# A new fixed order of the work in an attention and Hyena kernel on one Trainium2 core

## Chip, cores and metric

The kernel runs on one core of one Trainium2 chip. The metric is the device time of one execution in microseconds; smaller is better. Engines are named as in the profile: PE (TensorE, the matrix engine) with PEld (its weight loads), DVE (VectorE), ACT (ScalarE), POOL (GpSimd) and SP (SyncE, which here only issues DMAs).

## The reference

Softmax attention with one added to the denominator ("off by one"), then a Hyena layer on the joined heads. All inputs and outputs are float32; 8 batches, 12 heads, 448 positions, 64 values per head, so D = 768.

```python
def _attn_ref(q, k, v):
    scores = scale * np.matmul(q, k.transpose(0, 1, 3, 2))
    m = np.max(scores, axis=-1, keepdims=True)
    e = np.exp(scores - m)
    attn = e / (np.sum(e, axis=-1, keepdims=True) + np.exp(-m) + 1e-09)
    return np.matmul(attn, v)

def _moe_ref(x, w_proj, filter_fft, w_out):
    proj = x @ w_proj                       # [8, 448, 768] @ [768, 2304]
    x1, x2, x3 = proj[..., :D], proj[..., D:2 * D], proj[..., 2 * D:]
    X2 = np.fft.rfft(x2, n=S, axis=1)
    H = np.fft.rfft(filter_fft, n=S, axis=0)[None, :, :]
    x2_conv = np.fft.irfft(X2 * H, n=S, axis=1)
    return (x1 * x2_conv * x3) @ w_out
```

## The kernel before

**Attention.** Two heads are a group; 48 groups, six for each batch, numbered g = 0 to 47. For a group PE makes the scores (L842, the last 64 keys L844), ACT takes the exponentials (L855, L861), PE multiplies with the values (L873, L881), DVE divides by the sums (L894, L896) and leaves `xb`, which is transposed to `xT`: for batch 0 on PE (L978), for the others by a DMA.

**Loads.** SP issues the loads of q, k and v, POOL casts them to bf16. The last 64 keys and values of all twelve heads of a batch come in one load for each of k and v, the *shared* keys and values, named `rests` (L484 for batches 0 and 1, L619 for the others; runs of 256 bytes). Batches 0 and 1 are *staged*: loads at L467 (q) and L472 (k, v), casts at L494 (k), L500 (q), L507 (v), L522 (shared keys, `ks`) and L527 (shared values), then transposes on PE (L533 for the shared keys, L535 for the others, L542 for the query), copied back by DVE or, for group 6, the first of batch 1, by ACT (L550, L561). Batches 2 to 7 are *loaded*: L633 and L654, casts, and DMA transposes of q and k (L603, L610).

**Weights.** They are loaded by DMAs that POOL issues and thus stand in POOL's queue among its casts: the filter (L736, L737, L740), the projection in four parts (L820: x1's 1152 KB, the two halves of x2's of 576 KB each, x3's of 1152 KB) and the output weights (L825).

**Hyena layer, per batch.** x2's projection for batches 0 to 2 is L1070. For batches 3 to 7 it is *turned*: matmuls L1092, copies back on DVE (L1103) and ACT (L1105), a DMA transpose (L1109); then the spectrum matmuls L1142 read the transposed tile. The product with the filter's spectrum is on DVE (L1160, L1166). The gates x1 and x3 are L1192 on PE, with ACT's cast L1204 and DVE's product L1207; the inverse transform is L1238, with L1247, L1256, L1258, L1267; the gated y is L1282 (`yT`, `yR`), and the output matmuls are L1006, copied by ACT (L1314) and stored by SP (L1322, L1325, L1328).

**The flag.** A check of all batches for scores too large ends in a matmul L1407 and a copy L1409; at L1547 every engine reads the result and branches. A fixed set of output tasks is kept back to be run after the branch, in the same program.

**What sets the order.** The whole kernel but the setup is given to a planner, class `Plan`, as 2034 tasks: engine, modelled cost, needs, buffers. The planner simulates the engines and the DMA queues, and so decides the order in which each engine's instructions are written, and which PSUM banks they take. If `plan.ORDER` is given, a task's place among its engine's tasks is the number that stands for it in that list, and the simulation may no longer reorder an engine's queue:

```python
want = self.ORDER[len(self.tasks)] if self.ORDER else want + self.SHIFT.get(part, 0.0)
...
for i, t in enumerate(queue[e][: 1 if self.ORDER else self.WINDOW]):
    if ready(t):
        break
```

The number `run` of a DMA task is its weight when the two issuing queues share the DMA engines in the simulation: a transfer goes on at `run / total` of the speed, where `total` sums over the two transfers at the heads of the queues. Weight DMAs have 52 to 115, loads of q, k and v have 50, transposes 0.2.

Between the modelled times of 3 and 36 us the planner also fills modelled gaps of PE with matmuls on a tile of zeros (L1484, *fillers*; 78 of them). 38 more (L1492) run at the start.

Of the kernel before, what the change touches and what calls it, by code (L numbers as in the profile page):

```python
# [41 lines left out]
class Plan:  # L42
# [35 lines left out]
    def add(self, eng, cost, want, emit, need=(), make=(), take=(), give=(), dma=0.0, run=256, n=1, after=0.0, begun=(), late=0.0, turn=False, part=None, keep=False, port=False):  # L78
        want = self.ORDER[len(self.tasks)] if self.ORDER else want + self.SHIFT.get(part, 0.0)
        self.tasks.append((want, len(self.tasks), eng, cost, emit, need, make, take, give, dma, after, run, n, begun, late, turn, keep, port or eng == "POOL" and not dma))  # L80
# [221 lines left out]
def kernel(  # L302
# [93 lines left out]
    def stage(g, at, n):  # L396
        o = g % 4 * ROOM + at
        return nf[:, o : o + n]


    plan = Plan(
        {
            "e": 6, "er": 2, "k0": 2, "q0": 2, "u": 1, "w": 1, "xf": 1,
            "x2": 1, "x2s": 1, "x2h": 1, "xs": 2, "t0": 2, "t1": 2, "yh": 1, "g": 1, "x1": 2, "cr": 2, "cw": 1, "cv": 2, "yT": 1, "yR": 1,
            "os": 3,
        }
    )
# [25 lines left out]
    def tau(i, frac=0.0):  # L433

        if i >= NHP * n_batches:
            return tau(i - 1, frac + 1)
        h = i % NHP + frac
        return ATT[i // NHP] + SLOT[i // NHP] * min(h, 3) + LATER[i // NHP] * max(h - 3, 0)
# [4 lines left out]
    def rows(x, b, hp):  # L443
        o = x[b, 2 * hp].offset
        return bass.AP(x.tensor, o, [[3 * DH, 128], [512 * DH, 2], [1, 3 * DH]])

    def shared(x, b):
        o = x[b].offset + 384 * DH
        return bass.AP(x.tensor, o, [[DH, 128], [2 * S * DH, NHP], [1, DH]])

    def staged(b):
# [3 lines left out]
        for hp in range(NHP):  # L455
# [6 lines left out]
            for n, (name, x, at, size) in enumerate(parts):  # L462
                src = stage(g, at, size)

                def load(name=name, x=x, src=src, hp=hp, g=g):
                    if name == "q":
                        (nc.sync if g else nc.scalar).dma_start(  # L467
                            src[0:SP].rearrange("p (u c) -> p u c", u=2),
                            q[b, 2 * hp : 2 * hp + 2].rearrange("u (p j) d -> p u (j d)", j=NST),
                        )  # L470
                    else:
                        nc.sync.dma_start(  # L472
                            src.rearrange("p (u c) -> p u c", u=2), rows(x, b, hp)
                        )

                need = [("c" + name, g - 4)] if g >= 4 else []
                old = g - 2 * NHP
                first = name == "q" and g == 0
                add("ACT" if first else "SP", 0.52 if first else 0.5, -21.0 if first else want + 0.1 * n, load, need=need,
                    make=[("s" + name, g)], after=hold, dma=0.92 if name == "q" else 0.69, run=50,  # L480
                    begun=[("i" + name, g)])
                if hp == 0 and name != "q":
                    add("SP", 0.5, want + (0.05 if name == "k" else SLOT[0] + 0.05) if b == 0 else want - RE1 + 0.1 * n,
                        lambda name=name, x=x: nc.sync.dma_start(rests[:, "kv".index(name)], shared(x, b)),  # L484
                        need=[("cr" + name, b - 1)] if b else (), make=[("r" + name, b)],
                        dma=1.14, run=50, begun=[("ir", b)])

                on_pool = g > 0
                eng = nc.gpsimd if on_pool else nc.vector

                def cast(name=name, src=src, hp=hp, g=g, eng=eng):
                    if name == "k":
                        T[g]["kn"] = t = k0s[g % 2]
                        eng.tensor_copy(  # L494
                            t.rearrange("p j (u d) -> p u j d", u=2),
                            src.rearrange("p (u j d) -> p u j d", u=2, j=3),
                        )
                    elif name == "q":
                        T[g]["qn"] = t = q0s[g % 2]
                        eng.tensor_copy(  # L500
                            t.rearrange("p j u d -> p u j d"),
                            src[0:SP].rearrange("p (u j d) -> p u j d", u=2, j=NST),
                        )
                    else:
                        sv = src.rearrange("p (u j d) -> p u j d", u=2, j=3)
                        for u in range(2):
                            nc.gpsimd.tensor_copy(  # L507
                                vn[b % 2][:, hp, 4 * u : 4 * u + 3, 0:DH], sv[:, u]
                            )

                T.setdefault(g, {})
                if name == "v":
                    add("POOL", 0.62, tau(g) + (1.0 if b == 0 else -4.0), cast,
                        need=[("sv", g)] + ([("V", old, 1)] if b >= 2 else []), make=[("cv", g), ("v", g)])
                else:
                    add("POOL" if on_pool else "DVE", (0.47 if name == "k" else 0.58) if on_pool else 0.42, tau(g) - 5.0, cast, port=True,
                        need=[("s" + name, g)] + ([("c" + name, g - 1)] if g else []), make=[("c" + name, g)], take=[(name + "0", g)])
            if hp == 0:
                for u in range(2):
# [5 lines left out]
                        need=[("rk", b), "zero ks"] + ([("T", NHP * b - 1 - h) for h in range(NHP)] if b else []), make=[("crk", b)])  # L525
                add("POOL", 0.56, tau(g) + 1.0,
                    lambda: nc.gpsimd.tensor_copy(vn[b % 2][:, :, 3, 0:DH], rests[:, 1]),  # L527
                    need=[("rv", b)], make=[("crv", b), ("vr", b)])
# [65 lines left out]
    def loaded(b):  # L594
# [22 lines left out]
        for n, (name, x) in enumerate((("k", k), ("v", v))):  # L617
            add("SP", 0.5, tau(i0) - lead[0] - 0.2 + 0.1 * n,
                lambda name=name, x=x: nc.sync.dma_start(rests[:, "kv".index(name)], shared(x, b)),  # L619
                need=[("cr" + name, b - 1)], make=[("r" + name, b)], dma=1.14, run=50)  # L620
        for u in range(2):
            c = slice(64 * u, 64 * u + 64)
            add("POOL", 0.52, tau(i0) - lead[1] - 0.2, lambda c=c: nc.gpsimd.tensor_copy(kn[c, :, 0, c], rests[c, 0]),
                need=[("rk", b)] + (["zero kn"] if b == NSTAGED else [("kT", i) for i in range(i0 - NHP, i0)]), make=[("crk", b)])
        add("POOL", 0.52, tau(i0) - lead[3], lambda: nc.gpsimd.tensor_copy(vn[b % 2][:, :, 3, 0:DH], rests[:, 1]),
            need=[("rv", b), ("V", i0 - NHP - 1, 0), ("V", i0 - NHP - 1, 1)], make=[("crv", b), ("vr", b)])

        for hp in range(NHP):
# [8 lines left out]
                need=[("cq", g - QS)] if n >= QS else [("cq", i0 - 1)] if n == 0 else [], make=[("sq", g)], dma=0.92, run=50)  # L637
# [5 lines left out]
                need=[("sq", g)] + ([("qT", g - NHP)] if b > NSTAGED else staged_done), make=[("cq", g)])  # L643
            if hp % few == 0:
                gs = range(g, g + few)
                add("SP", (1.22, 1.42)[few > 1], tau(g) - lead[6], lambda hp=hp: q_turn(hp), need=[("cq", i) for i in gs] + last,
                    make=[("qT", i) for i in gs], dma=(0.7, 1.43)[few > 1], run=0.2, late=-0.2, turn=True)
            for n, (name, x) in enumerate((("k", k), ("v", v))):
# [6 lines left out]
                    need=room, make=[("s" + name, g)], dma=0.69, run=50)  # L655
                sv = src.rearrange("p (u j d) -> p u j d", u=2, j=3)
                if name == "k":
# [4 lines left out]
                        need=[("sk", g)] + (["zero kn"] if b == NSTAGED else [("kT", g - NHP)]), make=[("ck", g)])  # L662
                    if hp % few == 0:
                        gs = range(g, g + few)
                        add("SP", (1.22, 1.42)[few > 1], tau(g) - lead[2], lambda hp=hp: k_turn(hp), need=[("ck", i) for i in gs] + [("crk", b)] + last,
                            make=[("kT", i) for i in gs], dma=(0.78, 1.49)[few > 1], run=0.2, late=-0.2, turn=True)
# [798 lines left out]
    with (  # L1465
# [48 lines left out]
        for b in range(n_batches):  # L1514
            if b < NSTAGED:
                staged(b)
            else:
                loaded(b)
        add("DVE", 0.5, tau(NHP * NSTAGED) - 30.0, lambda: nc.vector.memset(kn[:, :, 0, :], 0.0),
            need=[("c" + x, g) for x in "kqv" for g in range(NHP * NSTAGED - NHP, NHP * NSTAGED - 2)], make=["zero kn"])  # L1520
        for (part, ch), at in zip(LOADS, LOAD):
# [4 lines left out]
            elif ch is None:  # L1526
                add("POOL", 0.82, at, lambda part=part: wproj_load(part, None), make=[("w", part, 0), ("w", part, 1)], dma=4.9,
                    run=60, late=-0.34, after=at)
# [6 lines left out]
        for b in range(n_batches):  # L1535
# [3 lines left out]
            need=[("T", NHP * NSTAGED - 1), ("T", NHP * NSTAGED - 2)], make=["x2h pads"])  # L1539
# [6 lines left out]
    with (  # L1546
# [6 lines left out]
        for b in range(n_batches):  # L1553
            W["yT", b], W["yR", b // 2] = y, yr
            stable(b)
            plan = Plan(plan.size)
# [9 lines left out]
    with tc.manual_schedule(engines={E.PE, E.Pool, E.DVE, E.Activation, E.SP}):  # L1566
        plan = main
# [31 lines left out]
```

## Time and profile before

| | us |
|---|---|
| median of 3 runs | 383.2 |
| lowest and highest | 382.7, 383.39 |
| the profiled execution | 381.13 |
| its span | 379.4 |
| PE busy | 364.5 (96%) |
| ACT busy | 264.0 (70%) |
| DVE busy | 260.4 (69%) |
| POOL busy | 111.8 (29%) |

The mean granted clock of PE in the profiled execution is 0.988 of full speed. The page and the views of the trace come from this one execution. In groups of instructions the numbers stand in this order: count (x), busy time in us, mean ns of one instruction from its start to its end (matmuls overlap, so busy time divided by the count is what one adds), idle time ahead of them on the engine and what ended it. In the timeline a row has the start, the length, the engine, the line, the operation and in brackets the idle time ahead with its releaser. Queue positions below are counted in the instructions as compiled.

### The profile page before, as it was taken

How to read it: one execution, taken by the hardware profiler on the slowest of the kernel's cores; microseconds unless marked ns; L12 is line 12 of the kernel's file. 1: busy time of each engine (PE TensorE's matmuls, PEld its weight loads, DVE VectorE, ACT ScalarE, POOL GpSimd, SP SyncE). 2: the span in 40 equal slices, each digit the busy share in tenths (PEclk: the TensorE clock that was granted, in tenths of full speed). 3: DMA queues.
4: the chain of work that ended last, by engine and by line, in shares of the span. 5: the costliest groups of instructions: out<-in, count | busy, mean ns of one | idle time of the engine just before them, and what ended most of it. 6: DMA issues, size and time to landing. Idle time of an engine off the chain costs nothing. (4 is left out here: it accounts for less than half of the span.)

```text
span 379.4 us, 9372 instructions
## 1 busy us (share of the span) xinstructions
PE 364.5 (96%) x3622; PEld 219.4 (58%) x3622; DVE 260.4 (69%) x676; ACT 264.0 (70%) x455; POOL 111.8 (29%) x240
## 2 busy tenths in 40 slices
PE   8878999999999999999999999999989999999995
PEld 6656666556755675655465545655545555555553
DVE  6465778966699668684685778695476855748770
ACT  4884887776877767886687567777868875446343
POOL 4834632423533373364116232430023000000000
PEclk9996999999999999999999999999999999999998
DMA  8999994999989999999999999997664044433035
GB/s 214 255 237 248 233 227 98 173 170 216 216 192 259 219 271 215 238 167 248 215 199 272 224 172 219 278 211 160 99 182 113 11 58 112 124 84 85 1 129 169
DMA packets 132450, 68.41 MB, mean 180 GB/s; under 512 B 88813, under 2 KB 129200, under 8 KB 132400
## 3 DMA queue, kind: packets, MB, share of 16 engines
q1 hardware_dynamic: 127680, 62.11, 73.1%
q0 software_dynamic: 4480, 5.41, 8.4%
q8 instruction: 29, 0.48, 0.5%
q10 hardware_dynamic: 240, 0.23, 0.2%
q14 instruction: 21, 0.17, 0.1%
HBM read 43.86 MB, written 11.01 MB: 145 GB/s over the span
## 5 line engine op out<-in xcount | busy, mean ns | idle before, releaser
L855 ACT ACTIVATE e<-psum 128x896 bf16<-128x896 f32 x144 | 128.3, 922 | 20.9 <-PE psum L842 18.9
L1192 PE MATMUL psum<-xT,wproj_bf 128*128 128x448 bf16 x576 | 122.1, 352 | 0.4 <-DVE g L1207 0.4
L1192 PEld LDWEIGHTS <-wproj_bf 128*128 128x128 bf16 x576 | 54.1, 98 | 45.8 <-issue 2.8
L1006 PE MATMUL psum<-wout_bf,yT 128*128 128x384 bf16 x288 | 53.1, 326 | 0.4 <-DVE yT L1282 0.4
L881 PE MATMUL psum<-vn,e 128*128 128x65 bf16 x1152 | 47.6, 195 | 0.0
L639 POOL CAST nat<-nat 112x512 bf16<-112x512 f32 x36 | 24.2, 674 | 73.7 <-DMA nat<-in_q_dram 70.4
L881 PEld LDWEIGHTS <-e 128*128 128x128 bf16 x1152 | 42.4, 98 | 5.2 <-issue 0.2
L1204 ACT CAST x<-psum 128x448 bf16<-128x448 f32 x48 | 25.5, 537 | 23.9 <-PE psum L1192 22.3
L842 PE MATMUL psum<-qT,kT 64*128 64x448 bf16 x288 | 41.2, 357 | 0.6 <-ACT e L855 0.4
L1160 DVE TENSOR_TENSOR t<-xs,hrs 113x768 bf16<-113x768 bf16 (+1 forms) x64 | 36.5, 592 | 6.4 <-ACT xs L1154 6.3
L1154 ACT CAST xs<-psum 113x384 bf16<-113x384 f32 (+1 forms) x64 | 29.2, 487 | 16.3 <-PE psum L1142 13.5
L1207 DVE TENSOR_TENSOR g<-x,psum 128x448 bf16<-128x448 bf16 x48 | 29.5, 617 | 15.9 <-PE psum L1192 12.2
L1314 ACT COPY osb<-psum 128x384 f32<-128x384 f32 x54 | 25.1, 486 | 19.7 <-PE psum L1006 14.9
L1006 PEld LDWEIGHTS <-yT 128*128 128x128 bf16 x288 | 27.1, 98 | 19.9 <-DVE yT L1282 1.9
L1092 PE MATMUL psum<-xf,wproj_bf 128*128 128x452 bf16 x180 | 38.6, 356 | 0.0
L896 DVE TENSOR_TENSOR xb<-psum,den 128x512 bf16<-128x512 f32 x48 | 33.2, 691 | 1.7
L894 DVE TENSOR_SCALAR den<-psum 128x8 f32<-128x8 f32 x48 | 7.8, 164 | 33.9 <-PE psum L881 26.3
L671 POOL CAST vn<-nat 128x192 bf16<-128x192 f32 x58 | 23.2, 432 | 26.0 <-DMA nat<-in_v_dram 26.0
L861 ACT ACTIVATE er<-psum 128x448 bf16<-128x448 f32 x48 | 26.2, 553 | 6.8 <-PE psum L844 6.1
L1247 ACT CAST cr<-psum 128x452 bf16<-128x452 f32 x48 | 24.6, 546 | 6.4 <-PE psum L1238 5.9
L1070 PE MATMUL psum<-wproj_bf,xf 128*113 128x384 bf16 x144 | 26.2, 327 | 0.0
L1092 PEld LDWEIGHTS <-wproj_bf 128*128 128x128 bf16 x180 | 16.5, 96 | 16.1 <-issue 1.1
(129 smaller groups left out, 471.5 us busy)
## 6 DMA issues: line engine op xcount, KB each, us to landing
nat<-in_q_dram SPq DMA_DIRECT2D x47, 224.0 KB, 4.9
out_dram<-osb SPq DMA_DIRECT2D x21, 384.0 KB, 3.4
nat<-in_k_dram SPq DMA_DIRECT2D x41, 192.0 KB, 4.2
nat<-in_v_dram SPq DMA_DIRECT2D x41, 192.0 KB, 3.9
wproj_bf<-in_moe_w_proj_dram POOLq DMA_DIRECT2D x2, 1152.0 KB, 15.7
out_dram<-osb SPq DMA_DIRECT2D x12, 192.0 KB, 2.8
rests<-in_k_dram SPq DMA_DIRECT2D x8, 192.0 KB, 4.4
rests<-in_v_dram SPq DMA_DIRECT2D x8, 192.0 KB, 4.4
```

The costliest lines, as they stand in the source:

```text
L842: nc.tensor.matmul(sc[:, u, 0:S], kT[b % 2][c, hp, t, :], qT[b % 2][c, hp, :])
L855: nc.scalar.activation(to, of, AF.Exp, scale=SCALE)
L861: nc.scalar.activation(to, of, AF.Exp, scale=SCALE)
L881: nc.tensor.matmul(out_bank(u)[:, n, :], P["e"][1 + t][:, u * S + n * 128 : u * S + n * 128 + 128], vn[b % 2][:, hp, 4 * u + t, :], start= ...
L896: nc.vector.tensor_tensor(W["xb", b][:, hp].rearrange("p n (u d) -> p u n d", u=2), op[:, :, :, 0:DH], rec[:].unsqueeze(3).to_broadcast([1 ...
L1006: nc.tensor.matmul(ops[:n, :DCH], y[:, dt, 0:n], wout_bf[:, dt, ch * DCH : (ch + 1) * DCH], start=(dt == 0), stop=(dt == NDT - 1),)
L1070: nc.tensor.matmul(pps[:FQ, :DCH], W["xf", b][:, pg, kt, 0:FQ], wproj_bf[:, kt, D + ch * DCH : D + (ch + 1) * DCH], start=(kt == 0), stop= ...
L1092: nc.tensor.matmul(pps, wproj_bf[:, kt, D + dt * 128 : D + (dt + 1) * 128], W["xf", b][:, :, kt, 0:FQ], start=(kt == 0), stop=(kt == NDT - 1),
L1154: nc.scalar.copy(L["xs", par, ch][:K, pg % 2, :], L["Z", pg, ch][:K, :DCH])
L1160: nc.vector.tensor_tensor(t[:K], L["xs", par, ch][:K], h, op=ALU.mult)
L1192: nc.tensor.matmul(p[:, :S], wproj_bf[:, kt, 2 * part * D + dt * 128 : 2 * part * D + (dt + 1) * 128], xT()[:, kt, 0:S], start=(kt == 0), ...
L1207: nc.vector.tensor_tensor(g[:, dt, :], L["x1", dt], p[:, :S], op=ALU.mult)
```

## The change

Two things change. `plan.ORDER` is another list: 2034 numbers for the same tasks, nearly all of them different. And `run` goes from 50 to 22 for the loads of the shared keys and values, in both functions that make them. As the order is fixed, `run` has no say in it; it changes only the simulated times, by which banks and fillers are placed. The tasks, tiles, buffers and their sizes are the same. The new program has 61 fillers instead of 78.

```diff
-    plan.ORDER = (5, 9, 12, 826, 13, 17, 0, 6, 23, 8, 24, 38, 1, 11, 162, 2, 10, 25, ...
+    plan.ORDER = (8, 0, 12, 277, 7, 9, 1, 4, 26, 11, 18, 20, 5, 48, 226, 10, 13, 24, ...
...
                         need=[("cr" + name, b - 1)] if b else (), make=[("r" + name, b)],
-                        dma=1.14, run=50, begun=[("ir", b)])
+                        dma=1.14, run=22, begun=[("ir", b)])
...
-                need=[("cr" + name, b - 1)], make=[("r" + name, b)], dma=1.14, run=50)
+                need=[("cr" + name, b - 1)], make=[("r" + name, b)], dma=1.14, run=22)
```

What the new order does to the instructions of each engine, from the two compiled programs:

- SP, head: batch 1's shared keys go from 19th to 18th load, group 6's query from 20th to 21st, group 5's keys from 16th to 17th; the bytes are the same.
- POOL, head: the first two loads of L820 (x1's 1152 KB and x2's first 576 KB) come after ten casts instead of six, right behind the cast of group 5's keys. The other two loads of L820, neighbours before, are separated by a memset, three casts and L527.
- PE, head: 16 of batch 0's transposes L978 stand ahead of group 6's transposes instead of 4, and 13 fewer fillers.
- PE, batches 3 to 7: other matmuls are put between a half's last L1092 and its first L1142, more of them than before in nine of ten halves.
- PE, end: 14 matmuls of L1006 stand between L1407 and the branch.
- ACT, head: the load of the Exp table stands ahead of the first copy of the transposed keys.

2 lines of the change are left out of this document (1 added, 1 removed).

## The prediction

> **What bounds the kernel now.** I read the page first (busy shares, the slices, the clock), then TensorE's waits, then the head of the program in stretches as long as the clock's own steps, then its instructions there.
>
> ```profile
> PE 364.5 (96%) x3622; PEld 219.4 (58%) x3622; DVE 260.4 (69%) x676; ACT 264.0 (70%) x455; POOL 111.8 (29%) x240
> ...
> PEclk9996999999999999999999999999999999999998
> ```
>
> TensorE (PE) works for 364.5 of 379.4 us, and no other engine passes 70%. So a reordering can win only in two places: the 14.9 us in which PE does nothing, and the slice near 30 us in which its clock is 0.6 instead of 0.9 or more. Who is to blame for the first stands in PE's waits (total, times, longest):
>
> ```profile
> PE psum L542 <- POOL ldm L500: 2.1, 4, 0.8
> PE psum L533 <- POOL ks L522: 1.9, 1, 1.9
> PE psum L1142 <- DMA x<-nat: 1.3, 1, 1.3
> PE psum L1492 <- DVE idle L1480: 1.1, 1, 1.1
> PE psum L873 <- DVE g L1207: 0.8, 2, 0.4
> PE psum L1142 <- DMA x<-ldm: 0.7, 1, 0.7
> ```
>
> Two families stand out: PE transposes of shared keys and queries in the head (L533, L542), and the spectrum matmuls L1142, which wait for a DMA transpose of x2. The head by stretches (length, busy time of each engine, granted clock, DMA share, GB/s):
>
> ```profile
> core 0: us, PE busy (x) PEld busy (x) DVE busy (x) ACT busy (x) POOL busy (x), PEclk, DMA share, GB/s
> 8.70:12.10 3.40, 2.30 (x34) 1.81 (x32) 1.54 (x4) 2.92 (x7) 2.43 (x7) 1.00 1.16 264
> ...
> 25.80:29.20 3.40, 1.39 (x19) 0.85 (x16) 2.23 (x5) 2.66 (x5) 1.30 (x2) 1.00 1.14 234
> 29.20:32.60 3.40, 2.65 (x28) 1.97 (x28) 0.15 (x1) 1.02 (x2) 1.48 (x4) 0.50 1.22 233
> 32.60:36.00 3.40, 3.40 (x39) 2.36 (x33) 3.33 (x8) 2.27 (x3) 1.54 (x3) 0.50 1.17 272
> ```
>
> Between 25.8 and 29.2 PE works 1.39 of 3.40 us; for the two stretches behind it the clock is 0.50. A stretch with 2.30 of 3.40 busy is not followed by that. So PE loses 2.01 + 0.75 = 2.76 us idle, and then does 2.65 + 3.40 = 6.05 us of work at half speed, which at full speed is half as much: 3.0 us more. The head has 5.8 us to give. What it waits for, by the timeline:
>
> ```profile
> 16.75 1.72 POOL L820 DMA_DIRECT2D wproj_bf<-in_moe_w_proj_dram  x2
> ...
> 19.01 0.52 POOL L494 CAST ldm<-nat 128x384 bf16<-128x384 f32 x1
> ...
> 27.72 1.36 POOL L522 CAST ks<-rests 64x384 bf16<-64x384 f32 x2 [5.86 <-DMA rests<-in_k_dram]
> ...
> 29.14 0.27 PE L533 MATMUL psum<-ident_bf,ks 128*128 128x128 bf16 x1 [1.94 <-POOL ks L522]
> ...
> 30.48 0.55 PE L542 MATMUL psum<-ident_bf,ldm 112*128 112x112 bf16 x4 [0.75 <-POOL ldm L500]
> ...
> 37.46 1.64 POOL L820 DMA_DIRECT2D wproj_bf<-in_moe_w_proj_dram  x2
> ...
> 42.41 2.12 PE L1070 MATMUL psum<-wproj_bf,xf 128*113 128x384 bf16 x12
> ```
>
> Batch 1's shared keys land late (issued at 13.56, 14.0 us), because from 16.75 two projection weights are in flight beside them, from the other queue (KB, us from issue to landing):
>
> ```profile
> wproj_bf<-in_moe_w_proj_dram POOLq DMA_DIRECT2D x1, 1152.0 KB, 14.2
> ...
> wproj_bf<-in_moe_w_proj_dram POOLq DMA_DIRECT2D x1, 576.0 KB, 18.5
> ...
> rests<-in_k_dram SPq DMA_DIRECT2D x1, 192.0 KB, 14.0
> ...
> wproj_bf<-in_moe_w_proj_dram POOLq DMA_DIRECT2D x1, 1152.0 KB, 17.3
> wproj_bf<-in_moe_w_proj_dram POOLq DMA_DIRECT2D x1, 576.0 KB, 10.2
> ```
>
> **The head, step by step.** The new order puts the first two weight loads (L820) behind the cast of group 5's keys, now the 17th load of SP's queue, before the 16th. Here that cast is the L494 at 19.01, with 1.72 us of L820's issuing ahead of it on POOL. It could end earlier by that, were its load not one place later and more casts ahead of it: I put the issue of L820 at 19 to 22, middle 20.2 (an estimate from those rows), against 16.75. Batch 1's shared keys go from 19th to 18th on SP, the query of group 6 (batch 1's first) from 20th to 21st.
>
> What that gives the loads: 3.4 us without the weights, at 234 GB/s of which I count half as theirs (an estimate), is 0.40 MB more for SP's queue, two loads of 192 KB at 0.8 us each. So keys and query land about 2 us sooner: the keys by 25.6 instead of 27.56, and the casts of 1.36 + 0.61 us behind them end at about 28, instead of 30.42. On PE's side, 12 more of batch 0's transposes now stand ahead of group 6's, and 13 fewer of the idle filler matmuls:
>
> ```profile
> L978 PE MATMUL psum<-ident_bf,xb 128*128 128x128 bf16 x24 | 2.6, 250 | 0.0
> ...
> L1484 PE MATMUL psum<-idle 128*128 128x128 bf16 x78 | 6.4, 223 | 0.0
> ```
>
> 12 x 2.6/24 = 1.3 us of useful work more against 13 x 6.4/78 = 1.1 us of filling less. So of the 2.76 us of idle time at most one is left, in one stretch of the clock, and the clock stays. As the fillers stand only in time that is otherwise idle, the 17 fewer of the whole program save nothing.
>
> By this PE would be up to 5.8 us early. But the L1070 at 42.41 needs the second weight load. Before, the pair took 0.87 (half of L820's 1.72, the second being issued after the first) + 18.5 = 19.4 us from 16.75, landed at 36.1, and nothing waited for it; the later pair, from 37.46, took 0.8 + 17.3 = 18.1 us. An issue at 20.2 plus 18.1 to 19.4 is 38.3 to 39.6, with the issue's ends 37.1 to 41.4. I take L1070 at 39.0, the middle: 3.4 us sooner, bounds 1.0 and 5.3. What is late next is thus this weight, no longer the keys; it costs 1 us for each microsecond of issue. The other weight loads now go out apart, with casts of queries between them, so the next query needn't queue behind both; the page shows no wait for them before, and I count nothing.
>
> **The transposes of x2.** In batches 3 to 7 the projection of x2 is turned: L1092, a copy back, a DMA transpose, then L1142. Where it came late:
>
> ```profile
> 182.38 0.37 PE L1142 MATMUL psum<-x,ft 113*112 113x384 bf16 x1 [0.69 <-DMA x<-ldm]
> ...
> 277.11 0.37 PE L1142 MATMUL psum<-x,ft 113*112 113x384 bf16 x1 [1.30 <-DMA x<-nat]
> ...
> L842 PE MATMUL psum<-qT,kT 64*128 64x448 bf16 x288 | 41.2, 357 | 0.6 <-ACT e L855 0.4
> ...
> L881 PE MATMUL psum<-vn,e 128*128 128x65 bf16 x1152 | 47.6, 195 | 0.0
> ...
> L1092 PE MATMUL psum<-xf,wproj_bf 128*128 128x452 bf16 x180 | 38.6, 356 | 0.0
> ...
> L1192 PE MATMUL psum<-xT,wproj_bf 128*128 128x448 bf16 x576 | 122.1, 352 | 0.4 <-DVE g L1207 0.4
> ```
>
> The new order puts more of PE's other work between the last L1092 of a half and its first L1142. In batch 3's first half, for one, 6 more L1092 and 12 more L881: 6 x 38.6/180 + 12 x 47.6/1152 = 1.3 + 0.5 us. In batch 5's second half 6 more L1192 and 4 more L842: 6 x 122.1/576 + 4 x 41.2/288 = 1.3 + 0.6 us. Every half of batches 3 to 7 but one gains between 1 and 4 us; the exception, batch 6's second, has over 10 left. The two waits, 0.69 and 1.30 us, are smaller than the added cover: 2.0 us less. Bounds 0.5 (if the transposes themselves take longer behind a busier queue) and 2.0.
>
> **What else moves.** In the middle the other engines' queues keep nearly the same sequence: 0, within 1 us either way (PE's two waits for L1207 sum to 0.8 and could double or go). At the end, the flag matmul has only 14 L1006 between it and the branch:
>
> ```profile
> 360.35 0.16 PE L1407 MATMUL psum<-one,bad 128*1 128x1 bf16 x1
> ...
> 369.98 2.18 PE L1006 MATMUL psum<-wout_bf,yR 128*128 128x384 bf16 x12
> ```
>
> Here 9.6 us lie between the two and PE doesn't stop; 14 x 2.18/12 = 2.5 us must now cover the flag's way. No row times it: it costs between 0 and 9.6 - 2.5 = 7.1 us. I take 0, as one number's copy and reading is short beside 2.5 us; the far end is the third rival's.
>
> **Sum:** 3.4 + 2.0 = 5.4 us less. The profiled execution took 381.13 us (span 379.4 and 1.7 around it), so 375.7 in its frame; it lies 2.1 us under the median of 383.2, from which I forecast 377.8. Own range: 374.9 (head 5.3, turns 2.0, the middle 1.0) to 382.7 (head 1.0, turns 0.5, the middle losing 1.0); these ends together are unlikely, and I give it 375.5 to 381.
>
> **Rivals.**
> First, *the clock falls again, now ahead of L1070*. If PE is done early and waits 2 us or more for the weight, the stretch looks like 25.80:29.20, and 6 us of work at half speed cost 3.0 again: the head nets only 0.4 us, the turns stay, 383.2 - 0.4 - 2.0 = 380.8. For it: PE could be there at 42.4 - 5.8 = 36.6, 2.4 us before the weight. Against: the idle time must fall into one stretch of 3.4 us, and 12 transposes plus fillers are to be run in it. The stretch with 2.01 us idle says that two microseconds are enough. [...] Chance 0.14.
>
> Second, ending slower: *the weights become the wait*. With the head's 17 loads slower than I reckon, POOL's queue, which is in order, holds L820 behind casts that wait. From an issue at 42.41 - 18.7 + 2.0 = 25.7 on, the turns' gain is used up; at 27, L1070 comes at 45.7, 3.3 us late, with a long idle time ahead of it and so 3.0 us of half clock behind it: 383.2 + 3.3 + 3.0 - 2.0 = 387.5; without the clock's fall 384.5. For it: POOL waited 5.86 us for a load in this very stretch. Against: that load stood three places behind the one that counts, which was there by 19.01. Chance 0.18.
>
> Third, also slower: *the flag's way or a new wait in the middle* takes 6 us or so (up to 7.1): 383.2 - 5.4 + 6 = 383.8. Against: nothing on PE waits there now. Chance 0.09.
>
> Fourth, *nothing comes of it*: gains and new waits cancel, 383. Chance 0.05.
>
> **The numbers.** The forecast keeps 0.54. A measurement of this kernel tells about 0.2%, 0.77 us, from no change. Faster: 0.54 + 0.12 of the first rival = 0.66; same: 0.02 + 0.05 = 0.07; slower: 0.27. The range goes from 375.3, nearly the forecast's outer end, to 385, which takes in the first, third and fourth rivals and the milder half of the second.
>
> **What would show it.** Right: L533 and L542 of group 6 without a wait of over 1 us, clock 1.00 from 26 to 40 us, L820 issued at 19 to 22, L1070 at 37.1 to 41.4, no L1142 waiting for a DMA. Wrong: a clock of 0.50 anywhere before 45 us, PE idle over 2 us ahead of L1070 or a first L1192 for want of weights, L820 after 24, waits for L1547 on PE, or new waits for `xT<-xb` or x2 after 100 us.

## The result

| | old order | new order |
|---|---|---|
| median, us | 383.2 (5 runs, 382.04 to 384.15) | 376.37 (5 runs, 375.65 to 377.04) |
| profiled execution, us | 381.13 | 376.26 |
| its span, us | 379.4 | 374.5 |
| its mean granted clock | 0.988 | 0.997 |

The ratio is 0.9825, with a 95% interval of 0.98 to 0.9851. The forecast was 377.8 in a range of 375.3 to 385.

The page after (busy time by engine, the clock in 40 slices):

```profile
PE 359.4 (96%) x3605; PEld 216.4 (58%) x3605; DVE 260.8 (70%) x676; ACT 262.2 (70%) x455; POOL 109.6 (29%) x240
...
PEclk9999999999999999999999999999999999999999
```

PE is still the bound. It is busy for 5.1 us less, though it has only 17 matmuls fewer, fillers of 1.4 us; most of the rest is what the old program's work at half speed had cost (3.0), and the slice of 0.6 is gone. PE's waits (total, times, longest):

```profile
PE psum L844 <- ACT e L855: 1.8, 2, 1.6
PE psum L1006 <- ACT osb L1314: 1.4, 1, 1.4
PE psum L535 <- POOL ldm L494: 1.2, 2, 0.8
PE psum L1492 <- DVE idle L1480: 1.1, 1, 1.1
PE psum L978 <- DVE xb L896: 1.0, 2, 0.6
PE psum L842 <- DMA kT<-nat: 0.7, 1, 0.7
```

No L533 and no L1142 is left in it. The two largest in their place are waits that the old trace did not have: L844 for an exponential, and L1006 for an output copy behind the branch.

The head, as windows of the same times as before:

```profile
25.80:29.20 3.40, 2.61 (x32) 1.70 (x32) 3.09 (x9) 2.84 (x5) 1.20 (x2) 1.00 1.15 233
29.20:32.60 3.40, 3.40 (x57) 2.35 (x56) 2.87 (x10) 3.13 (x6) 1.00 (x3) 1.00 1.20 213
32.60:36.00 3.40, 3.31 (x49) 2.00 (x45) 2.93 (x11) 2.63 (x7) 1.67 (x5) 1.00 1.23 222
```

The clock is 1.00 throughout. What keeps the mean at 0.997 lies behind PE's last matmul, which ends at 369.1: from 372.5 to the end of the trace the clock stands at 0.50 with nothing for PE to do. A mean clock therefore says little about a single fall of 3.4 us, and the stretches are read instead wherever a trace is at hand. POOL's queue, and PE at the step for which the second weight load is needed:

```profile
18.59 1.73 POOL L820 DMA_DIRECT2D wproj_bf<-in_moe_w_proj_dram  x2
...
22.14 1.06 POOL L522 CAST ks<-rests 64x384 bf16<-64x384 f32 x2
```

```profile
37.33 2.11 PE L1070 MATMUL psum<-wproj_bf,xf 128*113 128x384 bf16 x12
```

L1070 begins at 37.33 instead of 42.41. So the head gave 5.1 us. How long this lead holds can be read by laying the two traces side by side at equal amounts of useful PE work (fillers left out): 5.1 us at the end of the head, 4.6 at 150 us, 5.5 just ahead of 200 us, 3.5 behind the wait at L844, 4.9 at 260, 6.4 behind the place of the old second L1142 wait, 7.5 at 362 us. The span is only 4.9 shorter: the last 2.6 us were lost again behind the branch.

### The profile page after: what moved, and what is told of

Read it like the earlier page. It is cut to its first block, busy times and chain, and to the rows that moved or that the text cites. A ratio compares the mean times of both kernels' runs of the same rounds, so it can differ in the third digit from the quotient of the medians.

```text
span 374.5 us, 9317 instructions
## 1 busy us (share of the span) xinstructions
PE 359.4 (96%) x3605; PEld 216.4 (58%) x3605; DVE 260.8 (70%) x676; ACT 262.2 (70%) x455; POOL 109.6 (29%) x240
## 5 line engine op out<-in xcount | busy, mean ns | idle before, releaser
L1192 PE MATMUL psum<-xT,wproj_bf 128*128 128x448 bf16 x576 | 121.9, 352 | 0.2 <-DVE ldm L1103 0.2
L1192 PEld LDWEIGHTS <-wproj_bf 128*128 128x128 bf16 x576 | 54.0, 98 | 48.3 <-issue 4.6
L1006 PE MATMUL psum<-wout_bf,yT 128*128 128x384 bf16 x288 | 54.0, 326 | 0.2 <-DVE yT L1282 0.2
L881 PE MATMUL psum<-vn,e 128*128 128x65 bf16 x1152 | 46.7, 194 | 0.0
L881 PEld LDWEIGHTS <-e 128*128 128x128 bf16 x1152 | 41.3, 98 | 5.0 <-issue 0.6
L1160 DVE TENSOR_TENSOR t<-xs,hrs 112x768 bf16<-112x768 bf16 (+1 forms) x64 | 36.6, 601 | 10.8 <-ACT xs L1154 10.8
L842 PE MATMUL psum<-qT,kT 64*128 64x448 bf16 x288 | 41.1, 355 | 1.2 <-DMA kT<-nat 0.7
L1092 PE MATMUL psum<-xf,wproj_bf 128*128 128x452 bf16 x180 | 38.6, 356 | 0.0
L1006 PEld LDWEIGHTS <-yT 128*128 128x128 bf16 x288 | 27.2, 98 | 19.1 <-DVE yT L1282 1.1
L1204 ACT CAST x<-psum 128x448 bf16<-128x448 f32 x48 | 25.6, 536 | 15.9 <-PE psum L1192 15.1
L639 POOL CAST nat<-nat 112x512 bf16<-112x512 f32 x36 | 23.6, 663 | 40.4 <-DMA nat<-in_q_dram 28.7
L671 POOL CAST vn<-nat 128x192 bf16<-128x192 f32 x58 | 21.7, 404 | 38.2 <-DMA nat<-in_v_dram 33.3
L1247 ACT CAST cr<-psum 128x452 bf16<-128x452 f32 x48 | 24.4, 547 | 8.2 <-PE psum L1238 6.4
L1070 PE MATMUL psum<-wproj_bf,xf 128*113 128x384 bf16 x144 | 26.4, 327 | 0.0
L1092 PEld LDWEIGHTS <-wproj_bf 128*128 128x128 bf16 x180 | 16.4, 96 | 16.6 <-issue 1.5
```

The lines of the kernel that those rows point to most:

```text
L842: nc.tensor.matmul(sc[:, u, 0:S], kT[b % 2][c, hp, t, :], qT[b % 2][c, hp, :])
L881: nc.tensor.matmul(out_bank(u)[:, n, :], P["e"][1 + t][:, u * S + n * 128 : u * S + n * 128 + 128], vn[b % 2][:, hp, 4 * u + t, :], start= ...
L1006: nc.tensor.matmul(ops[:n, :DCH], y[:, dt, 0:n], wout_bf[:, dt, ch * DCH : (ch + 1) * DCH], start=(dt == 0), stop=(dt == NDT - 1),)
L1070: nc.tensor.matmul(pps[:FQ, :DCH], W["xf", b][:, pg, kt, 0:FQ], wproj_bf[:, kt, D + ch * DCH : D + (ch + 1) * DCH], start=(kt == 0), stop= ...
L1092: nc.tensor.matmul(pps, wproj_bf[:, kt, D + dt * 128 : D + (dt + 1) * 128], W["xf", b][:, :, kt, 0:FQ], start=(kt == 0), stop=(kt == NDT - 1),
L1160: nc.vector.tensor_tensor(t[:K], L["xs", par, ch][:K], h, op=ALU.mult)
```

## The experiments

Orders are described by what moves; in the code each is another list of 2034 numbers. Each kernel ran beside the old program, whose median is given with it (382.4 to 383.1). An execution of the old program took between 379.7 and 386.4 us, so a difference of less than a microsecond in medians of four executions says little, and less still between kernels that were measured in different series; where the text reads a wait, it is from the kernel's one profiled execution.

**run22: the share numbers alone.**

```diff
# old order; both places
-  dma=1.14, run=50
+  dma=1.14, run=22
```

> The old order with only the two share numbers changed (run = 22), so that at most the banks and the fillers differ. If the order does it all: 383.2, within 0.8, with the clock at 0.50 for some 7 us behind 29 us and a mean of 0.98 to 0.99. If the share numbers matter by the fillers they place: under 382. The executions' clocks also say whether the old program's 2.1 us between its profiled execution and its median lie in the clock: then the slower executions have a lower mean clock.

Measured: 381.37 (10 executions) against 382.91, ratio 0.9948 (0.9903 to 0.9994). By the time alone that is the second expectation (under 382), 1.5 us less than the old program; by the clock of the profiled execution (0.989) it is the first. The trace has 23 matmuls more than the old program, all fillers, and the executions a mean clock of 0.995 in their median against 0.991. The waits at L533 and L542 stand where they stood (1.5 and 1.6 us), and the clock still falls to 0.50 for 6.8 us in the profiled execution. So the new share numbers may give a small part, which the forecast had at nothing; rest_new, which has them too, gained nothing. The order does the rest.

**head_new and rest_new: the two halves alone.**

```diff
# head_new: tasks with a new number under 310 in the new order, the others behind them in the old
# rest_new: tasks with an old number under 310 in the old order, the others behind them in the new
```

> The new order up to its 310th task (about the first 45 us), the old one behind it. Theory (the head gives 5.1 us, the rest nets next to nothing, because 2.4 us won at L1142 and elsewhere are lost again at the flag): 378.1, or 376 if the old program's executions lose up to 2 us more in the head than the profiled one. L1142 waits of 0.5 to 1.3 us near 180 and 275 us remain. Rival (turns and middle carry most): above 380.

> The old order for its first 310 tasks, the new one behind. Theory: the wait for the shared keys and the half clock are back; L1142 has no wait; the flag costs 2.5 us at the end: 382.5 to 383.4. Rival (the turns' 2 us come through to the end, the flag being free): 381.2 or less.

Measured: head_new 379.09 (4 executions), ratio 0.9872 (0.9797 to 0.9946); rest_new 383.08 (10 executions), ratio 1.0018 (0.9984 to 1.0053). Both are within 1 us of what the theory said: the head alone wins, the rest alone nothing. PE's longest waits in head_new, where the old turns meet a PE that is early:

```profile
PE psum L978 <- DVE xb L896: 1.8, 3, 1.0
PE psum L1142 <- DMA x<-ldm: 1.6, 1, 1.6
PE psum L1142 <- DMA x<-nat: 1.4, 1, 1.4
```

and of rest_new:

```profile
PE psum L1006 <- ACT osb L1314: 2.5, 1, 2.5
PE psum L542 <- POOL ldm L500: 2.2, 3, 1.4
PE psum L844 <- ACT e L855: 1.9, 1, 1.9
```

The halves sum to 3.6 us, the whole is worth 6.5 to 6.8. In the profiled executions head_new keeps a lead of 3.0 us of the 4.7 that it has behind the head: the two waits at L1142 grew from 2.0 to 3.0 us, and an L1192 waited 1.0. The new rest is thus worth more behind the new head than alone. Why the two turns wait longer there stays open; run22, with the same old turns, waited only 0.2 us at L1142, so part of it is the spread of the executions.

**old_w_later: only the first two weight loads moved, in the old order.**

```diff
# POOL, old order
-  ... cast q(3), L820, L820, cast q(4), cast k(5), ...
+  ... cast q(3), cast q(4), cast k(5), L820, L820, ...
```

> The old order with only the first two projection loads (L820) moved on POOL from behind group 3's query to behind the cast of group 5's keys, two casts later; SP's order is the old one. Theory (these weights beside the shared keys make the keys late): L820 issued near 18, the keys 1 to 1.5 us sooner, less half clock, 1.5 to 3 us less than the old program's 382.9: 380 to 381.4. Rival (the keys' place behind group 6's keys, and the filter's load, make them late): L533's wait stays at 1.0 to 1.9 us, 382.4 or more.

Measured: 377.16 (4 executions) against 383.06, ratio 0.9871 (0.9801 to 0.9941); the profiled one 376.40. That is more than was expected, and nearly the whole gain by moving two instructions past two. L820 went out at 18.66 instead of 16.75, the shared keys landed at 23.6 instead of 27.6, group 6 no longer waited for them, and L1070 began at 37.99. The clock was 1.00 in the head, and the stretch that had 2.01 us idle has 0.07:

```profile
25.80:29.20 3.40, 3.33 (x52) 2.21 (x49) 3.01 (x8) 3.40 (x7) 1.45 (x3) 1.00 1.14 229
29.20:32.60 3.40, 3.27 (x46) 2.40 (x46) 3.33 (x8) 2.60 (x6) 2.13 (x3) 1.00 1.18 232
```

The old waits at L1142 (0.7 and 1.2) are all there.

**new_w_sooner: the same two loads moved back, in the new order.**

```diff
# POOL, new order
-  ... cast q(4), cast k(4), cast q(5), cast v(2), cast k(5), L820, L820, ...
+  ... cast q(4), L820, L820, cast k(4), cast q(5), cast v(2), cast k(5), ...
```

> The new order with only the two loads of L820 moved back on POOL, ahead of three casts of keys and query of groups 4 and 5 and one of values, so issued near 16.5 as in the old program. Theory (the weights' issue decides): group 6's keys and query land 2 us later, TensorE waits for them 1.5 to 2.5 us, the clock falls to 0.50 in some executions: 378 to 380. Rival (the keys' place, 18th on SP, decides): the keys still land near 20, no such wait, 376.4 within 0.8.

Measured: 375.07 (4 executions) against 383.06, ratio 0.979 (0.9735 to 0.9846). My theory of the weights fell here, and its rival held, with a time 1.3 us under the one that it named: L820 went out at 15.86, sooner than in the old program, and the shared keys landed at 18.15 all the same. L1070 began at 37.28, with the weight there at 35.83. The times of the keys' load, in the new order, in this kernel and in old_w_later (KB, us to landing; the old program took 14.0):

```profile
rests<-in_k_dram SPq DMA_DIRECT2D x1, 192.0 KB, 7.3
```

```profile
rests<-in_k_dram SPq DMA_DIRECT2D x1, 192.0 KB, 6.9
```

```profile
rests<-in_k_dram SPq DMA_DIRECT2D x1, 192.0 KB, 10.9
```

**old_keys_sooner: only the keys' place, in the old order.**

```diff
# SP, old order
-  ... load k(6), shared keys of batch 1, load q(6), ...
+  ... shared keys of batch 1, load k(6), load q(6), ...
```

> The old order with only one load moved on SP: batch 1's shared keys go ahead of group 6's keys, from 19th to 18th; the weights are issued as in the old program. Theory (the shared keys, in 768 runs of 256 bytes, crawl only if they fly beside the weights, so either way out of it will do): they land by 21 instead of 27.6, the wait at L533 is gone, the clock stays in most executions, 376.5 to 378.5. Rival (the weights' issue counts by itself, since they also hold up group 6's query): the query still waits for, 380 or more.

Measured: 375.93, 382.71, 382.81 and 388.18 us, too wide for a verdict. One execution has all of the gain, with a mean clock of 1.00; in the profiled one, the slowest, the keys still took 12.6 us (12.50 to 25.06) and PE waited 2.9 us at L533 and fell to half clock. The 388.18 is not the keys' alone: at 82 us PE waited another 3.5 us, for a DMA transpose of keys (L842), and the clock fell a second time, for 6.8 us from 81.2. One place on SP is therefore not enough to be safe: there the load ahead of the keys landed at 19.44, and in the new order at 18.09, with the filter's packets and then the weights' coming beside them. Either way out will do, if it gets the keys through in time: 1.4 us of SP's queue or the weights' later issue. For SP's queue this is read from the landings; no run took its lead away in the new order.

What makes the keys so slow is to be seen in the DMA view of the old program between 23 and 26 us (packets; then each queue's packets, MB, share of 16 engines):

```profile
DMA packets 596, 0.66 MB, mean 221 GB/s; under 512 B 56, under 2 KB 596, under 8 KB 596
...
q0 software_dynamic: 307, 0.47, 86.0%
q1 hardware_dynamic: 289, 0.19, 27.9%
```

In these 3 us the two queues got nearly equal numbers of packets, not of bytes: 307 of 1536 bytes for the weights, 289 smaller ones for SP, 56 of them under 512 bytes. Between 16 and 18 us and between 26 and 28 the counts are as near (199 and 191, 191 and 197). Counted by size in the same trace, 676 of the keys' 768 packets of 256 bytes went out between 19 and 21 us, while the filter's load ended and next to nothing of the weights was moving (by 21 us 443 packets of 1536 bytes had gone out, and the filter's 672 KB are 448 such). The other 92 went out behind them, at some 14 a microsecond beside some 100 of the weights, until 27. So it is the tail of the load that is slow; why these 92 came last, with later loads of SP's queue passing beside them, the trace does not say.

**warm and warm2: idle time filled, waits left, in the old order.**

```diff
# in group 6's transposes (g == NHP); warm has the first part only
+  for _ in range(30):
+      nc.tensor.matmul(bank(...)[:, 0:128], idle, idle)     # ahead of the shared keys' transpose
...
+  for _ in range(24):
+      nc.tensor.matmul(bank(...)[:, 256:384], idle, idle)   # ahead of the query's
```

> The old program with 30 matmuls on the tile of zeros ahead of group 6's transposes, where TensorE idles 1.94 us. The wait stays, the idle time doesn't. Theory (idle time of 2 us in a stretch of 3.4 us halves the clock): clock 1.00 from 26 to 40 us, 3.0 us less, 380.2. [...]

> The old program with idle matmuls ahead of both waits of group 6: 30 ahead of the shared keys' transpose, 24 ahead of the query's. The waits stay as they are, the idle time is gone. Theory (the clock falls behind a stretch of 3.4 us with 1.7 us or more idle, whatever the reason for it): clock 1.00 around 26 to 40 us in nearly all executions (mean clock 0.998 or more), 3.0 us less than the old program beside it, give or take 0.8. Rival (the clock falls for the load on DMA or other reasons): mean clock 0.99 as before, no gain.

Measured: warm 382.25 (10 executions) against 382.91, ratio 0.9976 (0.993 to 1.0022): inconclusive. It filled the first wait, but the second one grew to 1.74 us, and in the profiled execution the clock fell for one stretch. warm2, with both filled, 380.79 (10 executions) against 383.02, ratio 0.9955 (0.9922 to 0.9989). Nine of its ten executions have a mean clock of 0.998 or more, where the old program had 0.991 to 0.996 in 14 of 17 beside it. Two stretches of warm2:

```profile
26.00:29.40 3.40, 2.77 (x44) 2.31 (x42) 2.01 (x4) 2.06 (x4) 1.01 (x2) 1.00 1.16 231
29.40:32.80 3.40, 3.02 (x60) 2.60 (x58) 0.18 (x1) 1.14 (x3) 1.34 (x4) 1.00 1.22 237
```

The keys were late as ever (27.89); only the idle time was gone, and with it the half clock. So the fall follows from idle time (0.63 us in the first of these stretches, where the old program had 2.01 and fell). In the medians it is worth 2.2 us by itself, by the interval between 0.4 and 3.0. The profiled execution does not show that gain: PE came to L1070 at 41.56, 0.9 us sooner than in the old program, and there waited 1.75 us for DVE. The 3.0 us of half clock are thus not all on the path.

**new_w_later: the weights later still.**

```diff
# POOL, new order
-  ... cast k(5), L820, L820, cast v(3), cast k(6), L522, L522, ...
+  ... cast k(5), cast v(3), cast k(6), L522, L522, L820, L820, ...
```

> The new order with the two loads of L820 moved behind the casts of batch 1's shared keys, so issued near 23.2 instead of 18.6. Theory (from here on each microsecond of issue costs one at L1070, and idle time over 2 us halves the clock): L1070 at 41.7 instead of 37.3, 4.3 us, and 1.5 to 3 us of half clock behind the wait: 381 to 383.7. Rival (the loads before them profit, so that the weights fly faster and little is lost): 378.5 or less.

Measured: 379.93 (8 executions) against 383.06, ratio 0.9918 (0.9892 to 0.9945). L820 went out at 21.97, 3.4 us later than in the new order, the second weight landed at 40.0, L1070 began at 41.13, 3.8 later, and the median is 3.6 higher: a microsecond for a microsecond, and a time between the two expectations. The half clock behind the wait that I expected did not come, because the planner had put 47 fillers there:

```profile
35.58 2.79 PE L1484 MATMUL psum<-idle 128*128 128x128 bf16 x47
```

It came earlier, at 27.37, in this execution, and the two stretches around that show how little it takes (1.66 us idle):

```profile
23.96:27.37 3.41, 1.75 (x29) 1.11 (x26) 3.27 (x9) 1.49 (x3) 3.14 (x6) 1.00 1.19 244
27.37:30.79 3.42, 3.08 (x25) 2.18 (x24) 2.97 (x7) 2.49 (x5) 2.61 (x6) 0.50 1.14 241
```

**turn_short: the cover of two turns taken away, in the new order.**

```diff
# PE, new order
-  6 L1192, 6 L1092, 1 L844, first L1142 of batch 3, ...
+  first L1142 of batch 3, 6 L1192, 6 L1092, 1 L844, ...
...
-  12 L1192, first L1142 of batch 5's second half, ...
+  first L1142 of batch 5's second half, 12 L1192, ...
```

> The new order with only two L1142 moved forward on PE: batch 3's first one ahead of 6 L1192, 6 L1092 and one L844 (2.7 us), batch 5's first one of the second half ahead of 12 L1192 (2.5 us). In the new program's trace their transposes landed 0.2 and 1.55 us ahead of them. Theory (the waits at L1142 are cover alone, and what PE waits there is not made good later): waits of about 2.5 and 1.0 us at L1142, 376.4 + 3.5 = 379.9. Rival (a wait there is made good, because the waits behind it, such as the 1.55 us at L844 near 199 us, shrink by as much): 376.4 to 378.

Measured: 377.53 (4 executions) against 382.42, ratio 0.9871 (0.9851 to 0.9891). The waits are back, at the old places:

```profile
178.38 0.37 PE L1142 MATMUL psum<-x,ft 113*112 113x384 bf16 x1 [2.15 <-DMA x<-ldm]
```

and 0.72 us at 272.60. But they cost 1.2 us, in the median and in the span, not 2.9 (1.8 by the ratios to the old program beside each): laid beside the new program, this one is some 2 us behind after the first wait and only 0.3 behind after 200 us, since the wait of 1.55 at L844 is gone; the second wait leaves it 1.3 behind to the end. The rival had this right. A wait on PE ahead of a wait on ACT was paid once here.

**flag_early: the flag's matmul and copy some 10 us sooner, in the new order.**

```diff
# PE and DVE, new order: L1407 and L1409
-  ... L1006, L1407, 14 L1006, branch
+  ... L1407, ..., 18 L1006, branch
```

> The new order with only the flag's matmul L1407 and its copy L1409 moved some 10 us ahead on PE and DVE, to where the old order had them. Theory (SP needs 4.4 us from the flag's copy to its last event behind the branch, and ACT's copies wait for it; PE waited 1.4 us for them and the last store was 1.1 us later behind PE's end than before): 374.0 to 375.0. Rival (SP reaches the branch no sooner, because of its own stores ahead of it, or another copy is late next): 376.4 within 0.8.

Measured: 375.54 (4 executions) against 383.06, ratio 0.9806 (0.9748 to 0.9864); the profiled one has a span of 373.1 against 374.5. The medians, 0.8 us apart, would not show this by themselves. The wait at L1006 shrank from 1.39 to 0.35 + 0.64. Half of what the theory wanted: SP now reached the branch at 359.5, right behind its own last store, and still needed 3.3 us to come through. ACT's copies, in the new order and here:

```profile
365.06 2.56 ACT L1314 COPY osb<-psum 128x384 f32<-128x384 f32 x6 [6.04 <-SPq L1547]
```

```profile
363.50 2.18 ACT L1314 COPY osb<-psum 128x384 f32<-128x384 f32 x5 [4.38 <-SPq L1547]
```

**best: three moves on the new order.**

```diff
# POOL: L820, L820 as in new_w_sooner
# PE, DVE: L1407, L1409 as in flag_early
# ACT, batch 2's output copy (st 2, ch 0)
-  ... L1314, L855, L861, L855, L1204, ...
+  ... L855, L861, L855, L1314, L1204, ...
```

> The new order with three moves: the two loads of L820 issued near 16 as in new_w_sooner, the flag's matmul and copy 10 us sooner as in flag_early, and on ACT one output copy L1314 of batch 2 (it stood 2.5 us for a store, with an exponential behind it) put behind that exponential. Theory: 1.0 to 1.3 us less by the first, 0.8 to 1.4 by the second, 1.5 by the third: 372 to 373.5. Rival (the wait at L844 near 199 us moves to the next copy or exponential): 374 to 375.

Measured: 373.58 (6 executions, the lower five 372.4 to 376.5, the sixth 379.3) against 383.02, ratio 0.9762 (0.9705 to 0.982). By its median it beats both kernels; against the new order, whose ratio lies between 0.98 and 0.9851, the intervals still touch. The rival was half right: the wait at L844 for ACT is gone, and 1.4 us at an L844 5 us earlier have come for a DMA transpose of the queries:

```profile
193.98 0.35 PE L844 MATMUL psum<-qT,kT 128*128 128x448 bf16 x1 [1.36 <-DMA qT<-nat]
```

## Why the prediction was right, point by point

**The head, 3.4 us forecast, 5.1 measured.** The mechanism was right for the old program: the weights beside the shared keys, the wait, the half clock (old_w_later, warm2). What was mis-sized is the issue of L820: I put it at 19 to 22, and it came at 18.59, since POOL's casts ran just behind their loads. The flight, 18.4 us (18.59 to 37.04, both loads), is within my 18.1 to 19.4. So the weight, which I had as "late next", was in place 0.3 us ahead of L1070, and PE itself set 37.33. That is inside the bounds given, 37.1 to 41.4.

**"The keys by 25.6 instead of 27.56"** was wrong in size and, for the new order, in cause. They landed at 19.07. I counted half of the DMA's bytes as theirs; between 23 and 26 us of the old trace SP's queue had about half of the packets (289 of 596) but 0.19 of the 0.66 MB. And new_w_sooner shows that in the new order the weights' issue is not what saves them. What is left is SP's earlier queue, which no run took away by itself. Two changes were made at once, either of them enough, and I credited one. There was also room to spare: the keys' casts ended at 23.20, and group 6's L533 stood so far back in PE's new queue that it ran at 28.34.

**The clock stays**: right, since no stretch has much idle time, but not quite by the step given for it. PE's idle time did not shrink to "at most one" microsecond: it waits 2.5 us between 18 and 28 us (L535, L842, L978, L844). It falls in pieces over several stretches, with 1.26 us idle in the worst (24.4 to 27.8).

**The turns, 2.0 us**: right in the trace, with 0 left of 2.0 us, and right in cause (turn_short). What I missed is that a wait saved there can reappear behind ACT. The new one at 199 us comes from an output copy that waits 2.5 us for a store to free its buffer, with an exponential queued behind it:

```profile
197.74 0.48 ACT L1314 COPY osb<-psum 128x384 f32<-128x384 f32 x1 [2.54 <-DMA out_dram<-osb]
198.12 0.92 ACT L855 ACTIVATE e<-psum 128x896 bf16<-128x896 f32 x1
```

I had 0, within 1 us, for the middle; it lost 1.55 here and 0.7 at an L842, and got a little more than that back where the old program has small waits: of the lead of 7.5 us at 362 us the head and the turns make 7.1.

**The flag, 0 forecast, 2.6 us measured.** This is the step that failed. That one number's copy and reading are short beside 2.5 us was an estimate of mine that no row showed. I asked whether PE stops for the flag, and it does not: its first L1006 behind the branch follows without a gap. SP does, and ACT's copies wait for SP. From the flag's copy (360.43) to ACT's first copy behind the branch (365.06) it took 4.6 us, SP being the last one through. In the old order ACT stood there too, for 4.19 us, but PE lost nothing by it:

```profile
360.43 0.14 DVE L1409 CAST flag<-psum 1x1 int32<-1x1 f32 x1
```

```profile
370.49 1.24 ACT L1314 COPY osb<-psum 128x384 f32<-128x384 f32 x3 [4.19 <-SPq L1547]
```

In the new order PE ran into full PSUM banks:

```profile
365.97 1.14 PE L1006 MATMUL psum<-wout_bf,yR 128*128 128x384 bf16 x6 [1.39 <-ACT osb L1314]
```

and another 1.2 us were lost behind PE's end, where the copies and stores came later. I listed the queue of one engine at a branch that all of them cross. The flag's place in PE's queue is only a part of it: with the flag 10 us sooner, 1.4 of the 2.6 us came back (flag_early), and SP's own time at the branch stayed. The third rival named the place, but not the mechanism, and with 6 us was more than twice too dear.

**The frame.** The profiled executions differ by 4.9 us, the medians by 6.8. I carried one difference to the other without asking what the old program's executions differ by. Their mean clock was between 0.986 and 0.999, and the slower ones tend to have the lower clock (of 25, the eight under 0.9895 have a median of 383.4, the one at 0.999 took 380.0). But this does not explain the frame: the profiled execution, with 0.988, has one of the lowest clocks and yet took only 381.13. What makes it 2 us shorter than the median stays open. 3.4 + 2.0 came near the truth because the missed gain (1.7 in the head, some 2 in the frame) and the missed loss (2.6 at the flag) nearly cancel, and that is luck.

**The rivals.** The first (clock falls ahead of L1070) did not come, PE having no wait there. The second's price was borne out by new_w_later, at a microsecond for each of issue, without the half clock behind the wait. The fourth did not come either.

## What to carry to other kernels

Here a load in runs of 256 bytes took 6.9 to 7.3 us in the new order and 14.0 in the old one, where its tail went out beside the weights: get such a load through before the large packets start. Its place in its own queue (new_w_sooner) and the other queue's start (old_w_later, 10.9 us) are two ways to that, and either may be enough. Ask of every engine, not of the bound one alone, what a branch or a copy that waits for a buffer holds up: the price is paid at what stands behind it in that engine's queue (here 1.55 us of PE's time at L844 and 1.39 at L1006). And compare many executions, since one can be lucky: here the profiled one lay 2 us under its kernel's median.

## What was not expected of the hardware

The clock did not need one long gap to fall. It fell behind a stretch of 3.41 us of its own grid in which PE's idle time summed to 1.66 us or more: 1.66 (new_w_later), 1.76 (run22), 2.01 (old), 2.06 (warm), 2.47 (rest_new), and 2.71 and 3.02 (old_keys_sooner). It did not fall behind 1.44 (head_new, 23.7 to 27.1 us). By an estimate from these numbers the edge lies between 1.4 and 1.7 us, near half of the stretch. In rest_new it fell though no single wait was longer than 1.42 us. The grid is not fixed to the program: the falls in the head began between 27.4 and 30.5 us (one more, in old_keys_sooner, at 81.2), and some 1.9 us of idle time in head_new did no harm, as two stretches shared it (1.44 and 0.46). The half clock then lasted whole stretches: 3.4 us in rest_new, warm and new_w_later, 6.8 in the old program, run22 and old_keys_sooner. The old program's clock stood at 0.50 from 29.20 to 36.03 us and then at 1.00 to 377.36, which is 2 and 100 stretches of 3.41 us.

SP took 2.9 to 3.8 us from its comparison at the branch L1547 to its first event behind it, in the old order, the new one and flag_early alike, where ACT took 0.4. In that time the new program's trace has four packets on the queues that the DMA view calls `instruction` (0.04 MB), and the old one's has two (0.02 MB); what SP does in it the traces do not show, and no run tests it.
